# Pinned sums and transfers of the quarters moved to GpSimd's queue, in a retention and MLP kernel

## The chip, the cores and the metric

The kernel runs on one core of a Trainium2 chip. The metric is the device time of one execution in microseconds (us), taken as the median of several runs. The core has a matrix engine (TensorE, PE in the profile), VectorE (DVE), ScalarE (ACT), GpSimd (POOL) and SyncE (SP). SP, ACT and POOL can each issue DMA transfers, in the order of their own instruction streams.

## The reference, cut to what matters

A retention layer in recurrent form feeds an MLP with the quick GELU. B = 4, H = 8, S = 768, D = 64; 3072 tokens, d_model 512, d_ff 2048; all float32.

```python
for t in range(S):
    state = gamma * state + einsum('bhd,bhe->bhde', k[:, :, t], v[:, :, t])
    y[:, :, t] = scale * einsum('bhd,bhde->bhe', q[:, :, t], state)
x = y.transpose(0, 2, 1, 3).reshape(B * S, H * D)     # 3072 x 512
h = x @ w_in                                          # 512 x 2048
g = h * (1.0 / (1.0 + exp(-1.702 * h)))
out = g @ w_out                                       # 2048 x 512
```

## The kernel before, in words

The recurrence is computed in 24 chunks of 64 steps. `step(j, f)` scores chunk j and finishes chunk f = j - 1 on TensorE: L287 (scores, into `pa`), L295 (the state's update), L304 and L310 (the output, into `py`). L287 needs the transposes `qT` and `kT` of its chunk (L251, VectorE). What follows a step on VectorE is L316 (masked scores), L366 (state), L328 and L345 (the output into the tile `X`); on GpSimd L272 (`kd`, decayed k) and L357 (aged state).

Four chunks make a block of tokens; there are six blocks, m = 0 to 5. Each block has an up part, `x @ w_in` with the GELU, and a down part, `g @ w_out`. Both use a fast 2 x 2 matrix product of seven products in the place of eight, which needs sums of the operands' parts. These sums are what the change touches:

- `sums_g(m, p)` makes sums of g's parts for blocks 0 and 1: three on VectorE (L456, L457, L458) and a fourth on GpSimd (L459), for four pairs of parts. In block 1, g lies in `G`; in block 0, in the free parts of the tiles of w_in (`W1A`, `W1B`), `X` and `g0`.
- `sums_x()` makes the sums of X for a block's up part, on GpSimd (L440 to L443). They overwrite slots 2, 4, 5 and 6 of `X`. In the up part, a product with slot 5 comes third.
- `sums_w1(p)` makes sums of w_in's parts on GpSimd (L432 to L435) and saves two tiles to `W1D` in DRAM from SP's queue (L437).
- `inner_w2(i)` makes sums of quarters of part i of w_out, for i = 0 to 6: three dependent VectorE subtractions (L519) into slots 4 to 6 of `X`, then one transfer of 768 KB from these slots to `W2D[i]` in DRAM (L520). The next part uses the same slots, so its first subtraction waits for that transfer. `inner_w2_t3` (L525) makes one more sum in place. Blocks 2 to 5 read `W2D` back through GpSimd's queue (L541) for a second level of the fast product, `down49`.

The down part of blocks 0 and 1 is `down(m)`: a list of 28 units, four for each of the seven products. A unit is `part` (four matmuls at L705, eight records in the profile). Units 0 to 3 use part 0 of g, 4 to 7 part 1, 8 to 11 part 3. With units 8 to 11 `sums_g` is called; from unit 12 on, the products use the new sums: first part 0, then 3 and 2, and part 1 in units 24 to 27. `put` (L681) adds a finished product to a kept one and stores 256 KB of the output from GpSimd's queue (L682). `last_part` belongs to block 5 alone.

Between the units of block 1, the main loop puts the steps of the next chunks after units 5, 11, 16 and 21, and `sums_x` after the last of these; `sums_w1` after units 3, 11, 19 and 27. `INNER` says after which unit of which block `inner_w2` is called for each part of w_out.

The order on TensorE is that of the program, by hand (`manual_schedule`). On the other engines a scheduler may reorder what the program issues, by its own estimate of when operands are ready, unless an instruction is marked with `tc.keep_in_program_order`: marked instructions stay in the program's order. In the code before, nothing of `sums_g`, `inner_w2` or `put` is marked.

Of the kernel before, what the change touches and what calls it, by code (L numbers as in the profile page):

```python
# [28 lines left out]
def kernel(  # L29
# [29 lines left out]
    pe, act, dve, pool, sp = nc.tensor, nc.scalar, nc.vector, nc.gpsimd, nc.sync  # L59
# [11 lines left out]
    NB = NCH // CB  # L71
# [21 lines left out]
    W2D = [dram.tile([P, 3, NP // 2, P], F32, name=f"W2D{i}") for i in range(7)]  # L93
    W2 = const.tile([P, 7, NP, EH], F32, name="W2")

    X = const.tile([P, 7, 2, TH], F32, name="X")
# [15 lines left out]
    def w1(p):  # L112

        return (W1A, p) if p < NP // 2 else (W1B[p // 2 - 2], p % 2)
# [278 lines left out]
    def g(m, p, s):  # L393

        if m:
            return G[:, p:p + 2, s, :]
        if s < 3:
            t, q1 = w1(p)
            return t[:, q1:q1 + 2, 4 + s].rearrange("p a c f -> p a (c f)")
        return X[:, 4 + p // 2] if p < 6 else G0  # L400

    def g1(m, p, s):
        return g(m, p // 2 * 2, s)[:, p % 2]
# [25 lines left out]
    def sums_w1(p):  # L429
        t, q1 = w1(p)  # L430
        w = [t[:, q1:q1 + 2, s] for s in range(7)]
        pool.tensor_add(w[4], w[2], w[3])  # L432
        pool.tensor_sub(w[6], w[0], w[2])
        pool.tensor_sub(w[5], w[4], w[0])
        pool.tensor_sub(w[2], w[1], w[5])  # L435
        if p >= NP // 2:
            sp.dma_start(W1D[p // 2 - 2], W1B[p // 2 - 2])  # L437
# [15 lines left out]

    def sums_g(m, p):
        a = [g(m, p, s) for s in range(4)]
        dve.tensor_add(a[3], a[2], a[3])  # L456
        dve.tensor_sub(a[2], a[0], a[2])  # L457
        dve.tensor_sub(a[0], a[3], a[0])  # L458
        pool.tensor_sub(a[1], a[1], a[0])  # L459


    def up(d):
# [46 lines left out]
    def w2q(w):  # L509

        return [W2[:, w, u::2, e * P:(e + 1) * P] for u in range(2) for e in range(2)]

    def inner_w2(i):

        b11, b12, b21, b22 = w2q(ORDER[i][1])
        t = []
        for k, a in enumerate((b12, b22, b21)):
            t.append(X[:, 4 + k].rearrange("p c (d e) -> p (c d) e", e=P))
            dve.tensor_sub(t[k], a, t[k - 1] if k else b11)  # L519
        sp.dma_start(W2D[i].rearrange("p k d e -> p (k d e)"), X[:, 4:7].rearrange("p k c t -> p (k c t)"))  # L520

    def inner_w2_t3(i):

# [144 lines left out]
    def down(m):  # L668

        acc, kept = {}, {}  # L670
        b, t0 = m * CB // NC * 2, m * CB % NC * D
        rows = out.rearrange("(b t) (e c) -> e t b c", b=B, c=EH)[:, t0:t0 + TH, b:b + 2, :] \
            .rearrange("e (h p) b c -> h e p b c", p=P)

        def keep(name, tag, src):
            kept[name] = one.tile([P, 2, EH], F32, name=name, tag=tag)
            act.activation(kept[name], src, AF.Copy)

        def put(th, e, a, b):
            o = two.tile([P, 2, EH], F32, name="o")  # L680
            dve.tensor_add(o, a, b)  # L681
            (pool if m < NB - 1 else act).dma_start(rows[th, e], o)  # L682

        def last_part(d, halves={}):

            n = d // (NP // 4)
            if d % (NP // 4) == 0:
                halves[n] = ps.tile([P, EH], F32, name="pd", tag="xy"[n])
            for p in range(NP // 2 * (d % 2), NP // 2 * (d % 2 + 1)):
                pe.matmul(halves[n], g1(m, p, 1)[:, n * P:(n + 1) * P], W2[:, 3, p, :], start=(p == 0), stop=(p == NP - 1))  # L690
            if d % 2:
                o = two.tile([P, 2, EH], F32, name="o")
                dve.tensor_add(o[:, 0], halves[n], kept["t"][:, n])
                act.dma_start(rows[0, 1][:, n], o[:, 0])

        def part(key, sa, sb, new, last, d, then):
            if m == NB - 1 and key == "x2":
                last_part(d)
                return
            if d == 0 and new:  # L700
                acc[key] = ps.tile([P, 2, EH], F32, name="pd", tag=key[0])
            p0 = acc[key]
            for p in range(2 * d, 2 * d + 2):
                for n in range(2):
                    pe.matmul(p0[:, n, :], g1(m, p, sa)[:, n * P:(n + 1) * P], W2[:, sb, p, :],  # L705
                              start=(new and p == 0 and n == 0), stop=(last and p == NP - 1), skip_group_check=True)
            if d == NP // 2 - 1:
                then(p0)

        def then_p5(y):  # L710
            kept["t"] = one.tile([P, 2, EH], F32, name="t", tag="s1")
            dve.tensor_add(kept["t"], y, kept["u"])

        def then_p7(x):
            keep("vv", "s3", x)
            put(1, 0, acc["y1"], kept["vv"])
            put(1, 1, acc["y2"], kept["vv"])

        P_ = [("x", 0, 0, True, False, lambda x: keep("p1", "s1", x)),
              ("y0", 1, 2, True, True, lambda y: put(0, 0, y, kept["p1"])),  # L720
              ("y1", 3, 1, True, True, lambda y: None),
              ("x", 0, 5, False, False, lambda x: keep("u", "s2", x)),
              ("y2", 3, 4, True, True, then_p5),
              ("x", 2, 6, False, True, then_p7),
              ("x2", 1, 3, True, True, lambda y: put(0, 1, y, kept["t"]))]
        todo = []
        for n, (key, sa, sb, new, last, then) in enumerate(P_):
            for d in range(NP // 2):
                def unit(key=key, sa=sa, sb=sb, new=new, last=last, d=d, then=then, n=n):
                    part(key, sa, sb, new, last, d, then)  # L730
                    if n == 2:
                        sums_g(m, 2 * d)
                todo.append(unit)
        return todo

# [81 lines left out]
    for name, i in [("0a", 0), ("0b", 1)] + [(str(p), 2 * p) for p in range(1, NFF)]:  # L817
        n = Narrow(i)
# [37 lines left out]
    """.split():  # L856
        works[name]()
    ordered[0] = False
    INNER = [(0, 19), (0, 22), (0, 25), (1, 0), (1, 3), (1, 13), (1, 17)]
    for m in range(NB):  # L860
        between = []
        if m == 0:
# [26 lines left out]
        for n, unit in enumerate(down(m) if m < 2 else down49(m, *ring)):  # L889
            unit()  # L890
            if m == 0 and n < NP and n % 2:
                sums_w2(n - 1)
            if m == 0 and NP <= n < 3 * NP // 2:
                sums_w2_t3(2 * (n - NP))
            if m == 1 and n % 8 == 3:
                sums_w1(n // 4)
            if (m, n) in INNER:
                inner_w2(INNER.index((m, n)))
            if between and (n in (2, 5, 11, 16, 21) if m == 1 else n % 3 == (1 if m else 2)):
                between.pop(0)()  # L900
                if m == 1 and not between:
                    sums_x()
            if 1 < m < NB - 1 and n == 11:
                sums_x()
# [46 lines left out]
```

## Time and profile before

| what | value |
| --- | --- |
| median of 7 runs | 680.02 us (678.69 to 681.5) |
| profiled execution: its own time | 680.37 us |
| profiled execution: span, first to last instruction | 678.2 us |
| mean granted TensorE clock | 0.992 |
| TensorE busy / its weight loads | 97% / 84% of the span |
| VectorE / GpSimd / ScalarE busy | 65% / 25% / 23% |
| transfers of `W2D<-X` | 7 of 768 KB, SP's queue, 3.6 us to landing (median) |
| transfers of `out_dram<-o` from GpSimd | 20 of 256 KB, 3.7 us |
| transfers of `W1D<-W1B` | 2 of 1792 KB, SP's queue, 5.7 us |

The profile is of one execution, and its times run from the start of its span. The down part of block 0 runs from about 162 us to 212 us, that of block 1 from 212 to 275, and block 2 begins at 275. In a row of a timeline stand start, duration, engine, line, operation, what it writes and reads, and in brackets the idle time before it with what ended it. In a row of waits stand the waiting engine and line, whom it waited for, the sum in us, the number of times, and the longest.

### The profile page before, as it was taken

How to read it: one execution, taken by the hardware profiler on the slowest of the kernel's cores; microseconds unless marked ns; L12 is line 12 of the kernel's file. 1: busy time of each engine (PE TensorE's matmuls, PEld its weight loads, DVE VectorE, ACT ScalarE, POOL GpSimd, SP SyncE). 2: the span in 40 equal slices, each digit the busy share in tenths (PEclk: the TensorE clock that was granted, in tenths of full speed). 3: DMA queues.
4: the chain of work that ended last, by engine and by line, in shares of the span. 5: the costliest groups of instructions: out<-in, count | busy, mean ns of one | idle time of the engine just before them, and what ended most of it. 6: DMA issues, size and time to landing. Idle time of an engine off the chain costs nothing.

```text
span 678.2 us, 15331 instructions
## 1 busy us (share of the span) xinstructions
PE 655.6 (97%) x6502; PEld 568.9 (84%) x6502; DVE 438.2 (65%) x614; ACT 156.9 (23%) x313; POOL 170.5 (25%) x189
## 2 busy tenths in 40 slices
PE   6799999999999979799999999999999999999997
PEld 4688865747888858688999988999988999988997
DVE  4697881869856696145788255798254896254865
ACT  5565512321000000133200133200133200133210
POOL 3000000020279151300155700255700244500000
PEclk9799999999999999899999999999999999999999
DMA  9989832333414834512167573168573153502142
GB/s 185 207 201 224 207 104 107 124 93 47 71 58 180 308 75 110 142 28 74 62 167 174 126 250 102 50 169 180 110 252 103 49 156 111 217 32 94 47 156 94
DMA packets 143780, 88.97 MB, mean 131 GB/s; under 512 B 129472, under 2 KB 130752, under 8 KB 142688
## 3 DMA queue, kind: packets, MB, share of 16 engines
q1 hardware_dynamic: 134656, 48.33, 30.8%
q0 software_dynamic: 6752, 38.42, 15.9%
q10 hardware_dynamic: 2304, 1.25, 0.6%
q8 instruction: 51, 0.84, 0.6%
q14 instruction: 17, 0.14, 0.1%
HBM read 72.37 MB, written 15.47 MB: 130 GB/s over the span
## 4 chain that ended last, share of the span: by engine, by line
PE 91%; DVE 4%; DMA 2%; POOL 1%; issue 0%; ACT 0%; SPq 0%; POOLq 0%; ACTq 0%
PE pq L572 26%; PE px L469 16%; PE pd L705 12%; PE py L469 12%; PE ph L425 8%; PE ph L412 8%; PE pt L248 2%; PE pa L287 2%; PE py L310 2%; PE pa L295 2%; PE py L304 2%; DMA v_in<-in_v_dram 1%; DMA kn_in<-in_k_dram 1%; DVE G L457 1%; DVE G L458 1%; DMA W2D<-X 1%
## 5 line engine op out<-in xcount | busy, mean ns | idle before, releaser
L572 PE MATMUL pq<-W,G 128*128 128x128 f32 x672 | 80.2, 276 | 0.0
L572 PEld LDWEIGHTS pq<-W,G 128*128 128x128 f32 x672 | 77.6, 192 | 0.6
L541 POOL DMA_DIRECT2D ring<-W2D x28 | 15.5, 554 | 231.0 <-PE px L469 120.6
L469 PE MATMUL px<-X,W1A 128*128 128x256 f32 x256 | 61.6, 387 | 3.8 <-POOL X L442 3.8
L469 PE MATMUL px<-X,W1B 128*128 128x256 f32 x256 | 59.8, 379 | 0.0
L572 PE MATMUL pq<-ring,own 128*128 128x128 f32 x448 | 59.8, 276 | 0.0
L469 PEld LDWEIGHTS px<-X,W1A 128*128 128x128 f32 x256 | 49.3, 194 | 11.1 <-POOL X L442 4.2
L705 PE MATMUL pd<-W,G 128*128 128x256 f32 x224 | 50.4, 382 | 4.8 <-DVE G L458 4.8
L572 PEld LDWEIGHTS pq<-ring,own 128*128 128x128 f32 x448 | 54.5, 192 | 0.4
L469 PEld LDWEIGHTS px<-X,W1B 128*128 128x128 f32 x256 | 48.6, 190 | 6.6
L705 PEld LDWEIGHTS pd<-W,G 128*128 128x128 f32 x224 | 42.0, 190 | 11.8 <-DVE G L458 3.9
L469 PE MATMUL py<-X,W1A 128*128 128x256 f32 x192 | 45.4, 379 | 0.0
L469 PE MATMUL py<-X,W1B 128*128 128x256 f32 x192 | 45.4, 379 | 0.0
L391 ACT ACTIVATE G<-G 128x512 f32<-128x512 f32 x48 | 30.2, 630 | 52.0 <-DVE G L479 33.4
L469 PEld LDWEIGHTS py<-X,W1A 128*128 128x128 f32 x192 | 36.6, 191 | 5.1
L469 PEld LDWEIGHTS py<-X,W1B 128*128 128x128 f32 x192 | 36.5, 190 | 5.0
L487 DVE TENSOR_TENSOR t<-py,u 128x512 f32<-128x512 f32 x16 | 11.1, 692 | 41.2 <-PE py L469 41.2
L476 ACT ACTIVATE p<-px 128x512 f32<-128x512 f32 x16 | 9.6, 597 | 94.5 <-PE px L469 94.5
L412 PE MATMUL ph<-X,W1A 128*128 128x256 f32 x128 | 29.1, 383 | 1.1 <-DVE X L345 1.1
L572 PE MATMUL pq<-ring,G 128*128 128x128 f32 x224 | 29.6, 275 | 0.0
L572 PE MATMUL pq<-W,own 128*128 128x128 f32 x224 | 29.6, 275 | 0.0
L501 DVE TENSOR_TENSOR G<-G 128x512 f32<-128x512 f32 (+2 forms) x24 | 12.3, 514 | 25.7 <-ACT G L391 25.7
(202 smaller groups left out, 1180.8 us busy)
## 6 DMA issues: line engine op xcount, KB each, us to landing
ring<-W2D POOLq DMA_DIRECT2D x28, 768.0 KB, 4.9
W1B<-W1D POOLq DMA_DIRECT2D x6, 1792.0 KB, 11.1
W<-in_moe_w_in_dram SPq DMA_DIRECT2D x12, 512.0 KB, 6.2
W2D<-X SPq DMA_DIRECT2D x7, 768.0 KB, 3.6
W<-in_moe_w_out_dram SPq DMA_DIRECT2D x10, 512.0 KB, 4.5
out_dram<-o POOLq DMA_DIRECT2D x20, 256.0 KB, 3.7
v_in<-in_v_dram SPq DMA_DIRECT2D x64, 64.0 KB, 3.3
q_sq<-in_q_dram SPq DMA_DIRECT2D x128, 32.0 KB, 2.2
```

The source lines that it names most:

```text
L248: pe.matmul(p[n][HALF[r], s, :], x[n][:, HP * r + s, :], ident, start=True, stop=True)
L287: pe.matmul(pa[HALF[w], u, 0, s, :], kt[HALF[u], w, s, :], qt[HALF[u], w, s, :], start=True, stop=True)
L295: pe.matmul(pa[HALF[u], w, 1, s, :], kd[HALF[w], HP * u + s, :], vn[HALF[w], HP * u + s, :], start=True, stop=True)
L304: pe.matmul(py[HALF[o], u, 1, 2 * w + s2, :], old[HALF[u], w, 2 * s2 + o, :], qt[HALF[u], w, 2 * s2 + o, :], start=True, stop=True)
L310: pe.matmul(py[HALF[o], w, 0, 2 * u + s2 if f < 2 * CB else 2 * s2 + u, :], vn[HALF[w], HP * u + s, :], a[HALF[w], u, s, :], start=True, s ...
L391: pin(act.activation(g, h[:, i], AF.Gelu_apprx_sigmoid))
L412: pe.matmul(h[:, ab], w, X[:, 2 * th + c // 2, c % 2, :], start=(ab == 0 and c == 0), stop=(c == 3), skip_group_check=True)
L425: pe.matmul(h, w, X1[:, c // 2:4:2, c % 2, :], start=(c == 0), stop=(c == 3))
L469: pe.matmul(acc[:, u, :], t[:, q1 + u, sa, c, :], X[:, sb, c, :], start=(start and u == 0 and c == 0), stop=(stop and c == 1), skip_group_ ...
L541: pool.dma_start(c, W2D[i])
L572: pe.matmul(p0[:, j, :], a[:, d], w[:, d], start=(new and j == 0 and d == 0), stop=(d == NP // 2 - 1), skip_group_check=True)
L705: pe.matmul(p0[:, n, :], g1(m, p, sa)[:, n * P:(n + 1) * P], W2[:, sb, p, :], start=(new and p == 0 and n == 0), stop=(last and p == NP - ...
```

## The change

Five things are edited.

1. The three VectorE sums of `sums_g` are marked to stay in program order.
2. The fourth sum leaves `sums_g` for a new function, `sums_g_late`, which is called with units 16 to 19 in the place of units 8 to 11, and is marked too.
3. The subtractions of `inner_w2` are marked, and its transfers to `W2D` are issued from GpSimd in the place of SP.
4. The output transfers of `put` are marked.
5. In `INNER`, the last two parts of w_out are called after units 12 and 15 of block 1, before after 13 and 17.

```diff
     def sums_g(m, p):
         a = [g(m, p, s) for s in range(4)]
-        dve.tensor_add(a[3], a[2], a[3])
-        dve.tensor_sub(a[2], a[0], a[2])
-        dve.tensor_sub(a[0], a[3], a[0])
-        pool.tensor_sub(a[1], a[1], a[0])
+        tc.keep_in_program_order(dve.tensor_add(a[3], a[2], a[3]))
+        tc.keep_in_program_order(dve.tensor_sub(a[2], a[0], a[2]))
+        tc.keep_in_program_order(dve.tensor_sub(a[0], a[3], a[0]))
+
+    def sums_g_late(m, p):
+        a = [g(m, p, s) for s in range(2)]
+        tc.keep_in_program_order(pool.tensor_sub(a[1], a[1], a[0]))
...
-            dve.tensor_sub(t[k], a, t[k - 1] if k else b11)
-        sp.dma_start(W2D[i].rearrange("p k d e -> p (k d e)"), X[:, 4:7].rearrange("p k c t -> p (k c t)"))
+            tc.keep_in_program_order(dve.tensor_sub(t[k], a, t[k - 1] if k else b11))
+        pool.dma_start(W2D[i].rearrange("p k d e -> p (k d e)"), X[:, 4:7].rearrange("p k c t -> p (k c t)"))
...
             dve.tensor_add(o, a, b)
-            (pool if m < NB - 1 else act).dma_start(rows[th, e], o)
+            tc.keep_in_program_order((pool if m < NB - 1 else act).dma_start(rows[th, e], o))
...
                     if n == 2:
                         sums_g(m, 2 * d)
+                    if n == 4:
+                        sums_g_late(m, 2 * d)
...
-    INNER = [(0, 19), (0, 22), (0, 25), (1, 0), (1, 3), (1, 13), (1, 17)]
+    INNER = [(0, 19), (0, 22), (0, 25), (1, 0), (1, 3), (1, 12), (1, 15)]
```

In the changed program as it is built, the order on TensorE and ScalarE is the old one. On SP, the seven transfers to `W2D` are gone. On VectorE, from the end of block 0's sums of g on, the order is: L712; the groups of L519 for parts 0 to 4, with L681, L525, L316, L366, L251, L328 and L345 between them; L681; the twelve sums of block 1's g in one row (before, the groups of parts 0 to 5 stood ahead of them); six operations of the next step; the groups of parts 5 and 6; then the later steps. On GpSimd, transfers 0 to 4 stand between the sums of w_in (L433 to L435), outputs, L272 and L357; then come three of block 1's L459, transfers 5 and 6, the last L459, L272, X's sums L440 to L443, and the three last outputs of block 1, which stood ahead of X's sums before.

## The prediction

> **What bounds the kernel now.** I read three views in this order: engine shares and the chain, the waits of TensorE, then the timelines around each wait.
>
> ```profile
> PE 655.6 (97%) x6502; PEld 568.9 (84%) x6502; DVE 438.2 (65%) x614; ACT 156.9 (23%) x313; POOL 170.5 (25%) x189
> PE 91%; DVE 4%; DMA 2%; POOL 1%; issue 0%; ACT 0%; SPq 0%; POOLq 0%; ACTq 0%
> ```
>
> TensorE sets the time, so only its idle time can be won or added. In its waits, two rows belong to code that the change touches:
>
> ```profile
> PE pd L705 <- DVE G L458: 4.8, 4, 2.1
> PE px L469 <- POOL X L442: 3.8, 1, 3.8
> ```
>
> The first is block 1 waiting for the sums of g, the second block 2 waiting for X's sums. TensorE's timeline gives their places:
>
> ```profile
> 239.78 1.97 PE L705 MATMUL pd<-W,G 128*128 128x256 f32 x8 [2.11 <-DVE G L458]
> 242.69 1.99 PE L705 MATMUL pd<-W,G 128*128 128x256 f32 x8 [0.94 <-DVE G L458]
> 246.17 1.99 PE L705 MATMUL pd<-W,G 128*128 128x256 f32 x8 [1.49 <-DVE G L458]
> 248.44 3.72 PE L705 MATMUL pd<-W,G 128*128 128x256 f32 x16 [0.28 <-DVE G L458]
> ...
> 282.43 3.68 PE L469 MATMUL px<-X,W1A 128*128 128x256 f32 x8 [3.84 <-POOL X L442]
> ```
>
> A unit of eight matmuls takes 1.73 elsewhere; the last row takes 3.5 from its start to the next product. The view by stretches says why: the clock was 0.53 from 282.4 to 286.0, against 1.00 on both sides. So the second stall costs 3.84 + 1.78 = 5.6 us. Behind it stands SP's queue:
>
> ```profile
> 254.11 5.20 SPq L154 DMA_DIRECT2D k_sq<-in_k_dram  x8
> 259.35 0.45 SPq L520 DMA_DIRECT2D W2D<-X  x1
> ...
> 274.94 0.40 SPq L520 DMA_DIRECT2D W2D<-X  x1
> 278.67 1.26 POOL L440 TENSOR_TENSOR X<-X 128x512 f32<-128x512 f32 x1 [1.78 <-DMA W2D<-X]
> ```
>
> Quarter 5 was computed by 237.5, but its transfer stood behind rows of q and k until 259.35; quarter 6, computed at 267.1, went out at 274.94. X's slots 4 to 6 stayed in use until 278.53, and L440 could not overwrite them.
>
> **What the Trainium skill says.** "SBUF — State Buffer", Who interferes with whom: a VectorE instruction with two SBUF inputs and a GpSimd one that reads SBUF exclude each other. The trace agrees: beside L459 one L457 takes 1.64 us, alone 0.69. "TensorE: Matmul & The Clock Gate", What's actually happening: an idle window of about 3.4 us halves the clock. The trace agrees: 3.84 us idle was followed by 0.53, 2.11 us was not. "DMA: Bandwidth & Descriptors", Issuing engines are not separate DMA queues: transfers of all queues interleave on the same 16 engines. Here a W2D transfer took 3.3 us alone, and 4.7 and 5.6 to the next use beside the saves of W1D.
>
> **The change, part by part.** I follow the order in which the changed program has its instructions, on the clock of the trace before. Durations: successive VectorE operations 0.60, dependent ones 0.72; GpSimd sums 1.2, L272 and L357 1.04; GpSimd's issue of an output 0.75, of a 768 KB ring transfer 0.55; TensorE unit 1.73.
>
> *Price of a transfer on GpSimd's queue.* Before shows W2D writes only on SP: 3.3 to 3.6 uncontended. Ring reads of the same size on GpSimd's queue take 4.9 (the page), 256 KB outputs there 2.8 at best. The skill's DMA page (Anatomy of one DMA — SWDGE (gpsimd) path) prices 2.0 us + bytes / 436 GB/s, an estimate of 3.8. I take 3.7, bounds 3.3 and 4.9.
>
> *Group 0* (three L519) now stands behind L712, which is ready at 199.0; before, it began at 193.75. In turns with L272 and one L433 it ends at 203.0. Transfer 0: 203.1 (before 197.96).
>
> *Group 1* follows its landing at 206.9, in turns with L433, L434 and L435, and ends at 211.0. Transfer 1: 211.1 (before 206.0).
>
> *Group 2* follows at about 215. Transfer 2 also stands behind GpSimd's own work: 0.55 for transfer 1, two outputs 1.5, six sums 7.2, and some 2.0 waiting for VectorE's turns, 11.2 in all. Issue: 222.3 (before 214.2). VectorE is done 1.5 us earlier, so a landing slower by that much up to here costs nothing.
>
> *Transfer 2* now meets both W1D saves, 1.8 MB each or 4.7 us each at the 393 GB/s of the DMA rows. It shares, so 5.6 instead of 3.7 (bounds 4.4 and 7): group 3 runs from 228.0 to 230.1. Transfer 3: 230.1 (before 222.07). With the rest of W1D and the k and v rows I take 4.4 (bounds 3.6 and 5.5).
>
> *Group 4* starts at 234.6, with L251, L328 and L345 between its parts: kT of the next chunk is ready at 238.8. TensorE finishes unit 11 at 235.3 and wants that kT for L287: **3.6 us idle where before had none.** Its chunk ends at 240.9.
>
> *The sums of g* start after L525 and L681, at 240.0 (before 237.5). L459 no longer alternates with them: 4 x 2.05 = 8.2, plus 0.9 behind one L272, against 10.8 before. First sum 242.9, last 249.0. Units 12 to 16 run from 243.0 to 252.6 (before 252.09): **0.5 late.** So the early start is lost, but VectorE recovers most of it by running alone.
>
> *Quarters 5 and 6.* Six operations of the next chunk (3.6), then group 5 in turns with the three moved L459, ends at 256.7; transfer 5 at 256.8, free of SP's rows. It lands at 260.6, group 6 with one L525 takes 2.5, then L316, L366 and two L251 2.4: kT at 265.5. TensorE wanted it at 263.3, and its chunk ends at 267.85 (before 264.51): **3.3 late in all.** A half clock after the 3.6 us idle is covered by these 2.3 us of waiting; beyond them it may add up to 1.
>
> *X's sums.* Transfer 6 leaves at 263.2 and lands at 267; X of the last chunk is ready at 269.7; L440 to L442 end at 273.4. The three outputs now follow them. TensorE comes to its third product at 267.85 + 6 x 1.73 + 3.46 = 281.7: **no wait, 8 us of cover.** It starts 0.7 before the old 282.43, and runs 1.73 instead of 3.5.
>
> *At nothing:* L459 of block 0 has the same place as before; outputs released late have free buffers; the rows of k, v, q on SP start up to 4 us later but land before use, the k row of L272 near 269, still ahead of X's sums. From block 2 on, TensorE's order is unchanged and it had no idle time there.
>
> *Sum:* +3.3 for arriving later, -3.84 - 0.2 for the wait that goes, -1.78 for the clock: **-2.5 us.** The profiled span of 678.2 becomes 675.7 and its run of 680.37 becomes 677.9. That run lies 0.35 above the median of 680.02, so on the median: **677.5 us.**
>
> **The rivals.** A measurement of this kernel tells 0.2%, 1.4 us, from no change.
>
> *A: light landings.* Every transfer at SP's 3.3, and 4.0 beside W1D: group 4 comes 2.3 earlier, and so do all steps behind it; -4.9, **675.1 us.** For it: the write itself is only 2.0 us at 393 GB/s. Against: both prices known for GpSimd's queue are higher.
>
> *B: the stalls cancel.* Chain 1.5 to 3.5 longer, from one more turn per group and landings of 4.6: **680 us.** For it: seven groups, three landings and GpSimd's order in one chain.
>
> *C: slower, through GpSimd's queue.* The landings of transfers 2, 3 and 5 lie on one chain of VectorE, queue and TensorE, each microsecond passing one to one. Transfer 2 behind both W1D saves lands 3 later, and 1 more on each of 3 and 5 makes 5: +2.5, **682.5 us.** It decides from 2.5 us of extra landing in sum. For it: an output of 256 KB issued beside W1D at 220.70 took 4.8 us, against 2.8 to 3.7 elsewhere. Against: TensorE's cover ahead of X's sums is not touched.
>
> *D: no effect.* Pins only fix an order; if the order were the old one nothing would move. The order on VectorE and GpSimd does differ, so little is left: 680 us.
>
> **How the numbers follow.** Forecast 0.40 (-1.4 to -4.2), A 0.12, B 0.21, C 0.25, D 0.02. The forecast and A are faster: 0.52. B and D: 0.23. C: 0.25. The range takes A at its low end and C to its worked value, 674.9 to 682.5; the forecast alone spans 675.8 to 678.6.
>
> **What would show it.** Right: no wait of L469 for L442 and clock 1.00 near 282; new TensorE waits for L251 of some 3.6 at 235 and some 2.3 at 263; twelve sums of g in about 9 us from about 240; the fifth and later W2D transfers issued as soon as computed, at 238, 257 and 263. Wrong: a W2D landing above 5 without W1D beside it, groups of sums not turning by turns, L440 again waiting for a transfer, or a clock of 0.5 that lasts beyond 245.

## The result, and the profile after

The changed kernel takes **683.84 us** (median of 13 runs, 681.98 to 686.32), against 679.6 us for the kernel before on the same chip: a ratio of 1.0062, 95% interval 1.0047 to 1.0077. It is slower, by 4.2 us. The forecast of 677.5 had the sign wrong; the rival that came nearest is C.

The profiled execution took 684.39 us, with a span of 682.7. In this kernel the subtractions are L522, the transfers to `W2D` L523, the outputs L685, the down part's products L708 and the up part's L472. Block 1 begins at 211.30 here and at 212.54 before; predicted times are set 1.24 earlier where they are compared. From the page, engine shares and the chain:

```profile
PE 656.4 (96%) x6502; PEld 570.6 (84%) x6502; DVE 436.9 (64%) x614; ACT 157.1 (23%) x313; POOL 172.7 (25%) x196
PE 84%; DVE 6%; SPq 4%; DMA 3%; issue 2%; POOL 0%; DVEq 0%; POOLq 0%
```

TensorE does the same work in a longer span, and its share of the chain falls from 91% to 84%; VectorE, SP's queue, DMA and issue have more. Not all of this is the change: of the 4% of SP's queue, 12 us are the loading of the inputs in the first 15 us, which the change does not touch. So the loss is read from single waits. The waits of TensorE:

```profile
PE pa L287 <- DVE kT L251: 10.9, 2, 8.6
...
PE py L304 <- DVE X L345: 0.6, 1, 0.6
...
PE pd L708 <- DVE G L458: 0.3, 1, 0.3
```

The wait for X's sums is gone and that for the sums of g has shrunk from 4.8 to 0.3, as forecast. In their place stands the foretold wait for `kT`, but of 8.6 us instead of 3.6. TensorE's timeline:

```profile
242.95 1.13 PE L287 MATMUL pa<-qT,kT 64*64 64x64 f32 x32 [8.55 <-DVE kT L251]
...
246.90 9.79 PE L708 MATMUL pd<-W,G 128*128 128x256 f32 x40 [0.25 <-DVE G L458]
...
269.94 0.69 PE L287 MATMUL pa<-qT,kT 64*64 64x64 f32 x32 [2.39 <-DVE kT L251]
271.24 0.85 PE L304 MATMUL py<-qT,state 64*64 64x64 f32 x32 [0.61 <-DVE X L345]
...
272.87 11.68 PE L708 MATMUL pd<-W,G 128*128 128x256 f32 x48
...
287.84 1.89 PE L472 MATMUL px<-X,W1A 128*128 128x256 f32 x8
```

The last row is block 2's third product. It begins without a wait, but 7.4 us after its predicted place (281.7 - 1.24 = 280.46). Units 22 to 27, the row of 48 records, took 11.68 us; the same row took 10.63 in the kernel before. Why `kT` was late can be read on the queues and on VectorE. First the queues, GpSimd's and SP's:

```profile
218.57 3.25 SPq L437 DMA_DIRECT2D W1D<-W1B  x2
223.49 0.57 POOL L523 DMA_DIRECT2D W2D<-X  x1 [2.04 <-DVE X L522]
234.83 0.58 POOL L523 DMA_DIRECT2D W2D<-X  x1 [10.06 <-DVE X L522]
```

then the first subtractions of groups 2, 3 and 4 on VectorE, and below them GpSimd's sums beside the first of these:

```profile
215.50 4.82 DVE L522 TENSOR_TENSOR X<-W 128x512 f32<-128x512 f32 x1 [4.23 <-DMA W2D<-X]
232.39 0.69 DVE L522 TENSOR_TENSOR X<-W 128x512 f32<-128x512 f32 x1 [8.60 <-DMA W2D<-X]
238.50 0.69 DVE L522 TENSOR_TENSOR X<-W 128x512 f32<-128x512 f32 x1 [2.77 <-DMA W2D<-X]
```

```profile
216.06 1.27 POOL L435 TENSOR_TENSOR W1A<-W1A 128x512 f32<-128x512 f32 x1
217.28 1.26 POOL L435 TENSOR_TENSOR W1B<-W1B 128x512 f32<-128x512 f32 x1
218.51 1.26 POOL L434 TENSOR_TENSOR W1B<-W1B 128x512 f32<-128x512 f32 x1
```

Two things are to be seen. One subtraction of group 2 took 4.82 us, where one with nothing beside it takes 0.69: the three sums of GpSimd ran in a row, from 216.06 to 219.77, while it waited for its turn. And transfer 2, issued at 223.49 behind both saves, let group 3 begin only at 232.39: 8.9 us, where transfers 0 and 1 took 4.0. The DMA view of the stretch from 224 to 226 us, and below it that from 228 to 230 (packets, MB, share of the 16 engines' time):

```profile
q1 hardware_dynamic: 56, 0.79, 98.0%
...
q0 software_dynamic: 116, 0.71, 86.5%
q1 hardware_dynamic: 20, 0.07, 8.9%
```

q1 carries SP's saves, q0 GpSimd's transfers. Two us after its issue, transfer 2 had not moved a packet; it moved from 228 on, when the saves were all but through.

### The profile page after: what moved, and what is told of

Read it like the earlier page. It is cut to its first block, busy times and chain, and to the rows that moved or that the text cites. A ratio compares the mean times of both kernels' runs of the same rounds, so it can differ in the third digit from the quotient of the medians.

```text
span 682.7 us, 15337 instructions
## 1 busy us (share of the span) xinstructions
PE 656.4 (96%) x6502; PEld 570.6 (84%) x6502; DVE 436.9 (64%) x614; ACT 157.1 (23%) x313; POOL 172.7 (25%) x196
## 4 chain that ended last, share of the span: by engine, by line
PE 84%; DVE 6%; SPq 4%; DMA 3%; issue 2%; POOL 0%; DVEq 0%; POOLq 0%
PE pq L575 26%; PE px L472 16%; PE py L472 12%; PE ph L412 8%; PE ph L425 8%; PE pd L708 5%; PE pt L248 2%; DVE X L522 2%; SPq L154 2%; SPq L137 2%; PE pa L287 2%; PE py L310 1%; PE py L304 1%; PE pa L295 1%; DMA kn_in<-in_k_dram 1%
## 5 line engine op out<-in xcount | busy, mean ns | idle before, releaser
L472 PE MATMUL px<-X,W1A 128*128 128x256 f32 x256 | 59.9, 379 | 0.0
L472 PE MATMUL px<-X,W1B 128*128 128x256 f32 x256 | 59.8, 379 | 0.0
L472 PEld LDWEIGHTS px<-X,W1B 128*128 128x128 f32 x256 | 48.6, 190 | 6.6
L472 PEld LDWEIGHTS px<-X,W1A 128*128 128x128 f32 x256 | 48.3, 190 | 6.7 <-POOL X L442 0.3
L708 PE MATMUL pd<-W,G 128*128 128x256 f32 x224 | 51.5, 389 | 0.3 <-DVE G L458 0.3
L708 PEld LDWEIGHTS pd<-W,G 128*128 128x128 f32 x224 | 43.2, 195 | 7.2 <-DVE G L458 0.8
L472 PE MATMUL py<-X,W1A 128*128 128x256 f32 x192 | 45.4, 379 | 0.0
L472 PE MATMUL py<-X,W1B 128*128 128x256 f32 x192 | 45.4, 379 | 0.0
L472 PEld LDWEIGHTS py<-X,W1A 128*128 128x128 f32 x192 | 36.5, 190 | 5.0
L472 PEld LDWEIGHTS py<-X,W1B 128*128 128x128 f32 x192 | 36.5, 190 | 5.0
```

The lines of the kernel that those rows point to most:

```text
L472: pe.matmul(acc[:, u, :], t[:, q1 + u, sa, c, :], X[:, sb, c, :], start=(start and u == 0 and c == 0), stop=(stop and c == 1), skip_group_ ...
```

## The experiments

Four theories. **T1**: the saves of W1D hold the DMA engines, and transfer 2 waits on GpSimd's queue. **T2**: the turns between VectorE's groups and GpSimd's sums delay the issue of transfer 2. **T3**: the new order is the harm: group 4 stands ahead of `kT`. **T4**: GpSimd's queue is slow by itself. Each kernel was timed beside the kernel before; the ratios are to it.

**Both saves at the end of block 1.** The other engines' orders are untouched.

```diff
-        if p >= NP // 2:
-            sp.dma_start(W1D[p // 2 - 2], W1B[p // 2 - 2])
...
+            if m == 1 and n == 27:
+                for i in range(2):
+                    tc.keep_in_program_order(sp.dma_start(W1D[i], W1B[i]))
```

> The changed kernel with only the two saves of W1D moved from the middle of block 1 to its end on SP's queue; nothing else moves on any engine. T1 (the saves hold the DMA engines, and transfer 2 of W2D on GpSimd's queue waits until they have drained): transfer 2 lands in about 4 us in the place of 8.9, TensorE's wait for kT at 235 falls from 8.6 to about 3.7, and the kernel comes to about 679, -4.9 against the changed kernel, within 0.2% of the kernel before. T2 (the loss is the alternation of VectorE and GpSimd on the sums): no change, 684. T4 (GpSimd's queue is slow for such a write by itself): transfer 2 still takes over 6 us, 684.

Measured: 678.76 us, ratio 0.9992 (0.9979 to 1.0004), 5.1 us less than the changed kernel. VectorE's and TensorE's rows (two lines fewer, so the subtractions are L520):

```profile
227.43 0.69 DVE L520 TENSOR_TENSOR X<-W 128x512 f32<-128x512 f32 x1 [3.39 <-DMA W2D<-X]
```

```profile
237.96 1.13 PE L287 MATMUL pa<-qT,kT 64*64 64x64 f32 x32 [3.31 <-DVE kT L251]
...
264.93 1.14 PE L287 MATMUL pa<-qT,kT 64*64 64x64 f32 x32 [2.38 <-DVE kT L251]
```

Transfer 2, issued at 223.74, landed in 3.7 us; 8.55 us of wait became 3.31. So GpSimd's queue is not slow by itself (against T4), and taking the saves out of its way undoes the whole of the loss. That the ratio is 1.00 and not below says that something else eats what X's sums gave.

**One save moved.**

```diff
-        if p >= NP // 2:
-            sp.dma_start(W1D[p // 2 - 2], W1B[p // 2 - 2])
+        if p == NP - 2:
+            sp.dma_start(W1D[1], W1B[1])
...
+            if m == 1 and n == 27:
+                for i in range(1):
+                    tc.keep_in_program_order(sp.dma_start(W1D[i], W1B[i]))
```

> The changed kernel with the first of the two saves of W1D moved to the end of block 1; the second stays where it was, and VectorE, ScalarE and GpSimd keep their order. T1 (transfer 2 on GpSimd's queue waits until the saves have drained; its landing grows with the bytes still to be saved): one save of 1.8 MB is 4.7 us of DMA time, so transfer 2 lands in about 6.3 us, between the 3.7 without saves and the 8.9 with two; TensorE's wait for kT near 236 is about 6; 681 us, half way between 678.8 and 683.8. T4 (GpSimd's queue is slow by itself whenever anything runs beside it): 8 to 9 us again, 683 to 684. T3 and T2 are not touched by it: what they say is that the wait at 236 would stay near 8.6.

Measured: 686.99 us, ratio 1.0108 (1.0083 to 1.0133). The edit did not do what I had meant: on SP the moved save came to stand directly behind the other, and the two went out at 221.45 and 221.86 instead of 218.57 and some 221.5. The bytes ahead of transfer 2 became more, not fewer. As a dose it still serves. VectorE, group 3:

```profile
235.14 0.69 DVE L522 TENSOR_TENSOR X<-W 128x512 f32<-128x512 f32 x1 [11.37 <-DMA W2D<-X]
```

The issue is the same, 223.47; the landing 11.7 us instead of 8.9, and TensorE's wait for `kT` 11.29 instead of 8.55. The DMA view from 228 to 230, with the saves still under way:

```profile
q1 hardware_dynamic: 43, 0.60, 72.3%
q0 software_dynamic: 31, 0.19, 23.0%
```

So T1 holds in its size, later saves give a later landing, but not in its strict form. In both kernels the first packets of transfer 2 come at about 228, 4.5 us after its issue in the changed kernel and nearly 5 here, against about 1 us after it where no save runs. In the changed kernel the saves were all but through by then. Here they were not, and the two queues shared, at one to three. VectorE had nothing to run from 223.8 on in the changed kernel, so it is not its turns that held GpSimd there. What holds the first packet for so long was not found.

**The transfers back on SP's queue**, with the marks of the changed kernel.

```diff
-        pool.dma_start(W2D[i].rearrange("p k d e -> p (k d e)"), X[:, 4:7].rearrange("p k c t -> p (k c t)"))
+        sp.dma_start(W2D[i].rearrange("p k d e -> p (k d e)"), X[:, 4:7].rearrange("p k c t -> p (k c t)"))
```

> The changed kernel with the W2D transfers on SP's queue again, all pins and the moved fourth sum kept. T1: on SP's queue transfer 2 stands between the two saves, so it waits for one of them only: about 5 us to landing, kT at 235 some 3 us earlier, 680 to 682, less what transfers 5 and 6 lose again behind the rows of q and k (the kernel before lost up to 5.6 there). T4: every landing 0.5 us or more shorter than in the changed kernel, about 679. T3 (the order is the cause: with group 4 pinned ahead of the sums of g, any landing is on the path): not faster than the kernel before, since group 4 still stands ahead of the sums; 681 or more.

Measured: 682.27 us, ratio 1.0039 (1.0026 to 1.0053). SP's queue:

```profile
216.56 0.33 SPq L437 DMA_DIRECT2D W1D<-W1B  x1
217.30 0.32 SPq L523 DMA_DIRECT2D W2D<-X  x1
219.90 0.32 SPq L437 DMA_DIRECT2D W1D<-W1B  x1
```

Transfer 2 leaves earlier, behind the first save alone, and still needs 8.0 us to its next use at 225.29. So a long landing beside the saves is not a matter of GpSimd's queue alone. The old queue is no cure either, since the kernel still loses 2.7 us. But the run does not separate queue from order: some unmarked operations moved too, and `kT` now stands ahead of group 4 (229.18 against 232.97), so that TensorE does not wait for `kT` in block 1 at all. It waits 3.61 for the sums of g at 238.39, and 3.86 at block 2's third product, not for X's sums but for ScalarE's `p`, of which more below.

**The kernel before with the transfers on GpSimd's queue**, no order held.

```diff
-        sp.dma_start(W2D[i].rearrange("p k d e -> p (k d e)"), X[:, 4:7].rearrange("p k c t -> p (k c t)"))
+        pool.dma_start(W2D[i].rearrange("p k d e -> p (k d e)"), X[:, 4:7].rearrange("p k c t -> p (k c t)"))
```

> The kernel before, with only W_out's transfers moved to GpSimd's queue; no order is held. The scheduler then lets X's sums go ahead of the last outputs. T1: the transfer that goes out beside the saves of W1D lands in 8 to 9 us instead of 5.6, but in this kernel its group does not stand ahead of kT, so what is late is at most the sums of g: 1 to 3 us more at the waits for them; X's sums no longer wait, which gives 5.6. 675 to 679 us. T4: all landings beside other traffic near 5 or more, 680 or more. T3: the gain of X's sums alone, 675.

Measured: 682.09 us, ratio 1.0034 (1.0022 to 1.0046); a miss. TensorE:

```profile
237.03 1.14 PE L287 MATMUL pa<-qT,kT 64*64 64x64 f32 x32 [2.78 <-DVE kT L251]
239.82 1.13 PE L304 MATMUL py<-qT,state 64*64 64x64 f32 x32 [0.80 <-DVE X L345]
...
244.27 5.38 PE L705 MATMUL pd<-W,G 128*128 128x256 f32 x16 [2.47 <-DVE G L458]
252.58 1.99 PE L705 MATMUL pd<-W,G 128*128 128x256 f32 x8 [2.93 <-DVE G L458]
```

Transfer 2 went ahead of the saves here; transfer 3, issued at 222.95 behind them, needed 9.4 us, and the group that waits for it stands ahead of `kT` in this order too. That I had denied. The sums of g, not held, started later and took turns with group 5 and GpSimd; TensorE waited 5.7 us for them in all, against 4.8 in the kernel before. The wait for X's sums is gone, as in the changed kernel, and the gain is more than eaten up.

**The subtractions of groups 0 to 2 not held.**

```diff
-            tc.keep_in_program_order(dve.tensor_sub(t[k], a, t[k - 1] if k else b11))
+            op = dve.tensor_sub(t[k], a, t[k - 1] if k else b11)
+            if i > 2:
+                tc.keep_in_program_order(op)
```

> The changed kernel with the subtractions of groups 0, 1 and 2 no longer held; the scheduler then lets group 0 go ahead of the t of block 0 and the groups ahead of the outputs' sums, as in the kernel before. T1 with T2 (group 0 and GpSimd's turns bring transfer 2 behind the saves, and the saves then hold it): transfer 2 is issued near 214 and lands in 4 us; now transfer 3, issued near 223, meets the saves and lands in about 9, so group 4 ends near 234.5 and TensorE's wait for kT near 236 is 2 to 4 us instead of 8.6. 677.5 to 680. T3 (only group 4's place ahead of kT matters): the wait stays above 6, 682 or more.

Measured: 679.52 us, ratio 0.9996 (0.9982 to 1.0011): 4.3 us of the loss undone. VectorE, groups 2, 3 and 4, then TensorE:

```profile
208.69 1.57 DVE L522 TENSOR_TENSOR X<-W 128x512 f32<-128x512 f32 x1 [2.26 <-DMA W2D<-X]
...
218.30 2.01 DVE L522 TENSOR_TENSOR X<-W 128x512 f32<-128x512 f32 x1 [4.09 <-DMA W2D<-X]
...
232.21 0.69 DVE L522 TENSOR_TENSOR X<-W 128x512 f32<-128x512 f32 x1 [8.89 <-DMA W2D<-X]
```

```profile
236.91 0.87 PE L287 MATMUL pa<-qT,kT 64*64 64x64 f32 x32 [2.58 <-DVE kT L251]
```

Transfer 2 leaves at 214.68, ahead of the saves, and group 3 starts at 218.30. The 9.2 us behind the saves now fall on transfer 3. One group more has got through before them, and the wait is 2.58 instead of 8.55. The held order of the first three groups is thus what pushed transfer 2 behind the saves.

**GpSimd's sums of w_in out of the way**, with both saves late.

```diff
-            if m == 1 and n % 8 == 3:
-                sums_w1(n // 4)
+            if m == 1 and n in (20, 22, 24, 26):
+                sums_w1(n - 20)
```

(L432 to L435 are also marked, so that they stay there.)

> The kernel with both saves late, and the sums of W_in's second half (L432 to L435, sixteen on GpSimd) moved from the first units of block 1 to units 20 to 26. Only GpSimd's order differs from that kernel. T2 (the issue of transfer 2 is late because GpSimd's sums stand ahead of it and take the turns of VectorE's group 1 and 2): transfer 2 is issued near 218 instead of 223.7, one subtraction of 0.7 us no longer takes 4 to 5, transfer 3 leaves some 5 us earlier, and TensorE's wait of 3.3 for kT at 238 goes; the wait of 2.4 near 265 stays. 674 to 676 us. T3 (only group 4's place ahead of the sums of g matters): less than 1 us, 678 to 679.

Measured: 680.22 us, ratio 1.0014 (0.9999 to 1.003). TensorE:

```profile
263.44 1.13 PE L287 MATMUL pa<-qT,kT 64*64 64x64 f32 x32 [7.50 <-DVE kT L251]
283.40 3.49 PE L470 MATMUL px<-X,W1A 128*128 128x256 f32 x8 [2.66 <-ACT p L477]
```

T2's part came true: transfer 2 left at 215.68 (223.74 with the sums in their old place), no subtraction of groups 0 to 4 took over 1 us, and the wait of 3.31 near 238 is gone. The total missed: in their new place four of the sums (L432 to L435, from 248.26 to 254.2) stood ahead of transfer 5 on GpSimd. Group 5 was done at 248.85, its transfer was issued at 254.16 only, and for its landing group 6 and the last `kT` waited.

**Group 4 behind the sums of g**, saves where the changed kernel has them.

```diff
-    INNER = [(0, 19), (0, 22), (0, 25), (1, 0), (1, 3), (1, 12), (1, 15)]
+    INNER = [(0, 19), (0, 22), (0, 25), (1, 0), (1, 12), (1, 13), (1, 15)]
```

> The changed kernel with group 4 called after unit 12 of block 1 and group 5 after unit 13, in the place of units 3 and 12: group 4 then stands behind the sums of g and the next chunk's transposes do not wait for transfer 3. T3: kT is ready at about 237 in the place of 242.8, TensorE waits 2.7 there, the first sum of g is done at 241.4 in the place of 246.7, groups 4 to 6 follow later with a wait of about 2 at the last chunk; about 677 to 678, -6.4 against the changed kernel. T1 alone: the same 8.9 us landing remains, and only what stands behind it moves. T2: no change, 684.

Measured: 680.3 us, ratio 1.0011 (1.0 to 1.0022): 3.5 us better than the changed kernel, 2 to 3 short of what I expected. TensorE:

```profile
237.47 0.74 PE L287 MATMUL pa<-qT,kT 64*64 64x64 f32 x29 [2.71 <-DVE kT L251]
242.02 10.51 PE L708 MATMUL pd<-W,G 128*128 128x256 f32 x40 [1.26 <-DVE G L458]
...
283.74 1.97 PE L472 MATMUL px<-X,W1A 128*128 128x256 f32 x8 [1.46 <-ACT p L479]
```

Transfer 2 still takes 8.9 us, so group 3 alone makes `kT` late by 2.71; group 4 behind it had made the other 5.8 of the 8.55. That order as such is not new: in the kernel before, group 4 also began ahead of `kT` (226.75 against 230.64), and `kT` was in time. What is new is that group 4 waits behind a late transfer.

**Both: saves late and group 4 behind the sums of g.**

```diff
-        if p >= NP // 2:
-            sp.dma_start(W1D[p // 2 - 2], W1B[p // 2 - 2])
...
-    INNER = [(0, 19), (0, 22), (0, 25), (1, 0), (1, 3), (1, 12), (1, 15)]
+    INNER = [(0, 19), (0, 22), (0, 25), (1, 0), (1, 12), (1, 13), (1, 15)]
...
+                for i in range(2):
+                    tc.keep_in_program_order(sp.dma_start(W1D[i], W1B[i]))
```

> Both edits: the W1D saves at the end of block 1, and group 4 behind the sums of g. T1 and T3 together: group 3 ends near 229.6, the transposes follow at once, the sums of g run from 233.5 to 242.5 beside TensorE, which waits under 1 us in all of block 1, no half clock, no wait for X's sums; third product of block 2 at 272 to 274 in the place of 287.8: 669 to 671, -14 against the changed kernel. If one of the two causes is wrong, it comes out no better than the better single edit.

Measured: 674.37 us, ratio 0.9924 (0.9909 to 0.9939): faster than either kernel, but 3 above the 669 to 671 expected. TensorE's timeline, and the view by stretches from 260 to 266 (busy us, granted clock, DMA share, GB/s):

```profile
238.69 7.83 PE L706 MATMUL pd<-W,G 128*128 128x256 f32 x32 [0.71 <-DVE G L456]
259.20 0.69 PE L287 MATMUL pa<-qT,kT 64*64 64x64 f32 x32 [1.83 <-DVE kT L251]
260.51 1.13 PE L304 MATMUL py<-qT,state 64*64 64x64 f32 x32 [0.61 <-DVE X L345]
...
262.42 12.76 PE L706 MATMUL pd<-W,G 128*128 128x256 f32 x48
```

```profile
260.00:266.00 6.00, 5.49 (x73) 0.50 0.60 160
```

All that is left ahead of block 2 is 0.71 us for the sums of g and the last chunk's 1.83 + 0.61, with a half clock behind it that stretches the row of six units from 10.63 to 12.76. The two edits give 5.1 and 3.5 us alone and 9.5 together, nearly their sum: T1 and T3 take away different parts of one chain. The first alone undoes the loss of 4.2; with the second the kernel is 5.2 us faster than the one before.

**Then groups 5 and 6 at units 17 and 21.**

```diff
-    INNER = [(0, 19), (0, 22), (0, 25), (1, 0), (1, 12), (1, 13), (1, 15)]
+    INNER = [(0, 19), (0, 22), (0, 25), (1, 0), (1, 12), (1, 17), (1, 21)]
```

> The kernel with both saves late and group 4 behind the sums of g, with groups 5 and 6 four and six units later (units 17 and 21 instead of 13 and 15). T3 (a group of W_out's subtractions ahead of a chunk's kT makes TensorE wait, because the group waits for a transfer): the last chunk's waits of 1.8 and 0.6 us near 260 go and with them the half clock behind them; third product of block 2 near 273 instead of 278.5; 669 to 671 us. If X's sums are then late because transfer 6 leaves later, a wait of L470 for X appears, 672 to 674. If neither, the half clock near 260 had another cause: 674.

Measured: 678.93 us, ratio 0.9979 (0.9966 to 0.9992), its profiled run 676.76; a miss by 8. The last chunk's waits and the half clock there are gone, as expected. A new wait took their place. VectorE, ScalarE and TensorE:

```profile
276.59 0.69 DVE L682 TENSOR_TENSOR o<-pd,t 128x512 f32<-128x512 f32 x1 [7.97 <-DMA out_dram<-o]
```

```profile
277.39 0.60 ACT L477 ACTIVATE p<-px 128x512 f32<-128x512 f32 x1 [14.86 <-DVE o L682]
```

```profile
278.13 3.75 PE L470 MATMUL px<-X,W1A 128*128 128x256 f32 x8 [5.93 <-ACT p L477]
```

Read it backwards: the third product waits for `p`, `p` for the third `o` of block 1, that `o` for the first output to land and free its buffer, and that output was issued at 273.7 only, because the held order puts it behind X's sums on GpSimd. The third product begins about where it did in the kernel with groups 5 and 6 early (278.13 against 278.47), and then runs at half clock.

**The same with block 1's outputs on ScalarE's queue.**

```diff
-            tc.keep_in_program_order((pool if m < NB - 1 else act).dma_start(rows[th, e], o))
+            tc.keep_in_program_order((act if m in (1, NB - 1) else pool).dma_start(rows[th, e], o))
```

> The kernel with both saves late, group 4 behind the sums of g, and groups 5 and 6 at units 17 and 21, with block 1's four outputs on ScalarE's queue instead of GpSimd's (that of the later blocks is as it was). In the same kernel with the outputs on GpSimd's queue, TensorE waited 5.9 us for p of block 2, because the outputs stood behind X's sums, the third o waited for the first output to land, and p stands behind that o. If that is the cause, the wait goes and what comes next is X's sums, which end near 273.7 while TensorE wants its third product at 272: 1 to 2 us, and the half clock of 1.8 goes too. 670 to 672.5 us. If the outputs were not the cause, 677 to 679 as with GpSimd's queue.

Measured: **672.12 us**, ratio 0.9886 (0.9858 to 0.9913), the best of all. ScalarE and TensorE:

```profile
267.81 6.70 ACTq L683 DMA_DIRECT2D out_dram<-o  x3
274.62 0.60 ACT L477 ACTIVATE p<-px 128x512 f32<-128x512 f32 x1 [11.48 <-DMA out_dram<-o]
```

```profile
275.36 1.97 PE L470 MATMUL px<-X,W1A 128*128 128x256 f32 x8 [2.55 <-ACT p L477]
```

The outputs were the cause. A wait for `p` of 2.55 remains, since `p` now stands behind the third output in ScalarE's own stream; a wait of 1 to 2 had been expected there, but for X's sums.

**And the saves back in place**, with everything else of that kernel.

```diff
+        if p >= NP // 2:
+            sp.dma_start(W1D[p // 2 - 2], W1B[p // 2 - 2])
...
-                for i in range(2):
-                    tc.keep_in_program_order(sp.dma_start(W1D[i], W1B[i]))
```

> The same with the saves of W1D back where the changed kernel has them. T1: transfer 2 lands in 9 us again and group 3 ends 5 us later, but no chunk's kT stands behind group 4 any more; what is late is group 3 ahead of kT of the next chunk, 2 to 4 us of wait near 237 (2.7 with group 4 behind the sums of g and the saves in place). 673 to 676 us. If the saves do no more harm once group 4 is out of the way: 670 to 672.

Measured: 677.02 us, ratio 0.9963 (0.9947 to 0.9979), 1 us above the expected band. TensorE's wait for `kT` is 2.68 at 236.63, as expected. The saves alone cost 4.9 us in this kernel too.

## Why the prediction was wrong

**What held.** X's sums no longer wait and the clock is 1.00 there. The sums of g, running alone, took 9.0 us (243.90 to 252.91) where 8.2 + 0.9 was worked out. The six other transfers of the changed kernel landed in 3.6 to 4.3, the price taken being 3.7. TensorE's new waits are at the two places foretold, and the second was 2.4 against 2.3.

**The step that failed: "It shares, so 5.6 instead of 3.7 (bounds 4.4 and 7)."** Transfer 2 took 8.9, outside the bounds. The prediction leaned on the Trainium skill, "DMA: Bandwidth & Descriptors", Issuing engines are not separate DMA queues, that transfers of all queues interleave, and sized that by two transfers of the kernel before, 3 and 4, with 4.7 and 5.6 us to the next use. Those left on SP's queue 4.2 us after the first save (222.07 for 217.88) and 6.4 after the second (228.93 for 222.48), when the save ahead of them, 4.7 us long by the prediction's own figure, was nearly or wholly through. Neither was issued into two saves. The transfers do interleave, but late: nothing of transfer 2 moved for 4.5 us. The measurement decides: behind both saves, five kernels showed 8.9 to 9.4 us from issue to next use, and the one with later saves 11.7. Even on SP's queue, 0.7 us behind one save and ahead of the other, transfer 2 took 8.0. Moving the saves away gave back 5.1 us, more than the whole loss of 4.2.

**The second step: "Issue: 222.3".** On this clock 222.3 - 1.24 = 221.06 was forecast, and transfer 2 left at 223.49, 2.4 late. It came in three parts. Transfer 0 was 0.4 late, transfer 1 was 1.7 late (211.56 for 209.86), and between the two stood 11.93 us for the 11.2 of the sum. The 1.3 of group 1 have a plain part: two output sums of VectorE (L684, 0.6 each) stand between its subtractions, and the account of group 1 does not count them. Between transfers 1 and 2, the term "some 2.0 waiting for VectorE's turns" has its size by luck: GpSimd waited 2.04 us, for group 2 to be finished. Groups and sums did not take turns one by one. The sums went three at a time, one subtraction lasted 4.82, and so "VectorE is done 1.5 us earlier" did not come about. The page "SBUF — State Buffer", Who interferes with whom, calls the shared ports an exclusive lock and says that issue order decides who blocks. The trace agrees that one engine blocked the other; it also shows the blocked one losing three turns on end.

**The third: "A half clock after the 3.6 us idle is covered by these 2.3 us of waiting".** With 8.55 us of idle time there was more half clock (0.50 from 240 to 246, beyond the 245 given as the bound), and a second came where none had been foreseen, in the last chunk (0.50 from 272 to 275). The step and units 22 to 27 took 2.93 and 11.5 us there, against 2.40 and 10.5 in the kernel with one save moved, where waits of the same length left the clock at 1.00. So this half clock cost some 1.6.

The sum, at block 2's third product: 2.4 for the late issue of transfer 2, 3.3 for its landing, -0.7 for transfer 3 (3.67 instead of 4.4) and 0.3 for smaller terms bring units 12 to 16 to their end 5.3 late; the last chunk, some 1.6 of it by its half clock, adds 2.1. That is the 7.4 read above. Added to the forecast of -2.5 it makes +4.9. The profiled executions differ by 4.0 and the medians by 4.2; the difference of under 1 us I did not follow.

**Rival C** had the mechanism in words, place and first size: transfer 2 behind both saves, 3 later. It added 1 each for transfers 3 and 5, which did not come, and had no term for the late issue and the last chunk, which cost 2.4 and 2.1. It also "decides from 2.5 us of extra landing", and one landing passed that. It got 0.25 because I weighed an output of 4.8 us beside one save, the only evidence in the trace of before, as if it were typical of a transfer behind two.

**At nothing: "outputs released late have free buffers".** In the changed kernel the late outputs cost nothing, but only since TensorE was later still. Once the other delays were removed, they were the next wait: 1.46, 2.66, 3.86 and 5.93 us in four kernels. The forecast's own cover can be estimated at some 2.7 us. From the end of X's sums to the third product the chain of outputs took 4.4 (273.73 to 278.13, groups at units 17 and 21). The forecast's 273.4 is the end of L440 to L442; L443, another 1.2, also stands ahead of the outputs. So the product could not begin before some 279.0, and 281.7 was forecast.

## What to carry to other kernels

When an edit moves a chain of small transfers, write the large transfers of every other queue beside it on one clock, and ask which side of them each small one falls: here the transfer behind the saves took 5 us longer (8.9 against 3.7). Do not price a transfer behind large ones on another queue by sharing from its issue; bound it by the end of what is ahead plus its own time, which came within about 1 us of the landings in these runs. And when a stall is removed, follow the buffers of what was moved behind it, because the next wait (here an output's buffer behind X's sums) is already in the program.

## What the runs showed of the hardware that I had not expected

A transfer on GpSimd's queue, issued into a stream of two 1792 KB saves, moved its first packet about 4.5 to 5 us later in six kernels, where the saves were ending and where they ran for 4 us more alike; alone it took about 1 us. It is no fixed delay: in the kernel before, an output of 256 KB that was issued amid the first save (220.70) moved 2.3 us later. What causes it was not found.

The half clock does not follow from the length of idle time alone. After 1.83 + 0.61 us of idle in the last chunk the clock was 0.50 for the next 6 us in the kernel with both edits; after 1.85 + 0.61 us at the same place in the kernel with group 4 moved alone it stayed at 1.00. After 2.39 + 0.61 us it was 0.50 in the changed kernel, after 2.50 + 0.61 us 1.00 in the one with one save moved. The Trainium skill, "TensorE: Matmul & The Clock Gate", What's actually happening, has a free-running window of about 3.4 us, which would let two equal gaps differ, but an idle gap shorter than that window halved the clock here. Whether the small 64 x 64 matmuls of the step beside the gap count as idle no run decides.
